# Gate and up products by one level of Strassen's scheme in an adaLN + convolution + GLU kernel

## Chip, cores and metric

The kernel runs on one core of one Trainium2 chip. The metric is the device time of one execution in microseconds (us); the median of three runs of the kernel before is 601.48 us (601.07 to 602.88). A core has five engines with a queue each, which run in program order and wait for one another by semaphores: TensorE (PE, matrix products into PSUM), VectorE (DVE), ScalarE (ACT), GpSimd (POOL, which has no access to PSUM here) and SyncE (SP), whose queue starts the DMA transfers.

## What is computed

One block of an adaptive-layernorm network on 2048 rows of 448 channels, all in fp32: a layernorm with a learned scale and shift, a gated long convolution, a second layernorm with scale and shift, and a gated linear unit (GLU) with 1792 inner columns.

```python
h = _layernorm(x) * (1 + ca) + sa
x = x + ga * conv_block(h, k, v, shift_k, ssm_k, ssm_D)
h = _layernorm(x) * (1 + cb) + sb
g = h @ w_gate            # 2048 x 448 times 448 x 1792
u = h @ w_up
x = x + gb * ((sigmoid(g) * u) @ w_down)     # 1792 x 448
```

The convolution is done by products with Fourier tables; it is the same in both kernels. The change concerns the last three lines.

## The kernel before

**Layout.** The GLU's rows come in four row blocks of 512 (`n` = 0 to 3), its inner columns in seven groups of 256 (`j`, NGRP = 7), each of two halves of 128 (`f`). The normalised rows are transposed on TensorE (`norm_turn`, L730), so that channels lie on partitions: 448 channels are three tiles of 128 and one of 64. A product is `weights (128 channels x 128 columns)` times `x (128 channels x 512 rows)` into a PSUM bank of 512 columns.

**Precision.** Every operand is split into two numbers of TensorE's fast fp32 format, hi and lo (hi = a rounded copy, made by ACT; lo = value - hi, made by DVE). A product is then hi*hi + lo*hi + hi*lo: three matmuls for a full tile. The tile of 64 channels holds its hi part in the lower and its lo part in the upper 64 partitions, beside weights that are there twice, and needs two. So a gate or an up block of 128 columns takes 3 x 3 + 2 = 11 matmuls.

**gate_up** (L755) does the 22 matmuls of gate and up for one (j, n, f) into a pair of banks (PSUM tag `t`, two pairs in turn), then ACT takes the sigmoid of gate out of PSUM (L768), DVE multiplies it by up out of PSUM (L769), and h is split (hi by ACT L772, lo by DVE L773). **down** (L776) does 12 matmuls per 256 rows of the product with w_down (tag `y`, one pair) and DVE adds them to the result `x1` (L790); on the last group the result is stored (L792).

**Order of work.** The program is written out by hand: within `manual_schedule` each engine gets its instructions in the order of the calls. At L862 the blocks (j, n) are listed; for each block the two halves of gate/up follow each other, and after each half comes one down call of the block before. `ends` (L845) names small jobs that follow a half: loads of the next weights (`load_w`), their splits (`split_hi` L489 on ACT, `split_lo` L497 on DVE), row statistics (`ln2_stats` L408), normalising of later row blocks (`norm_rows` L717). w_down is multiplied by the output scale gb on POOL (`gate_raw` L484). Just ahead of the GLU, the last output of the convolution is multiplied by the gate and added to x (`gate` L355: a product and a sum per quarter); of the second half's four quarters all are done by DVE, the last two between GLU blocks (L846, L847).

## Time and profile before

| | before |
|---|---|
| runs, median (lowest to highest) | 601.48 us (601.07 to 602.88) |
| profiled execution, span from first to last instruction | 602.7 us |
| TensorE clock granted, mean | 0.994 |
| instructions | 7614 |
| ACT busy | 41% |
| DMA | 51.87 MB, mean 86 GB/s |

The profiled execution has no time of its own beside its span; the span lies within the range of the three runs and 1.2 us above their median. The page of the profile lists busy time by engine, the chain of work that ended last and groups of instructions by source line; the timeline lists the instructions of an engine in order with start and duration. A group is named by what it writes and reads: gu is the PSUM tile of gate and up, d that of down, xt the transposed rows, wt the split weights, hh and hl the two parts of h, x the result. L numbers are lines of the kernel before.

### The profile page before, as it was taken

How to read it: one execution, taken by the hardware profiler on the slowest of the kernel's cores; microseconds unless marked ns; L12 is line 12 of the kernel's file. 1: busy time of each engine (PE TensorE's matmuls, PEld its weight loads, DVE VectorE, ACT ScalarE, POOL GpSimd, SP SyncE). 2: the span in 40 equal slices, each digit the busy share in tenths (PEclk: the TensorE clock that was granted, in tenths of full speed). 3: DMA queues.
4: the chain of work that ended last, by engine and by line, in shares of the span. 5: the costliest groups of instructions: out<-in, count | busy, mean ns of one | idle time of the engine just before them, and what ended most of it. 6: DMA issues, size and time to landing. Idle time of an engine off the chain costs nothing.

```text
span 602.7 us, 7614 instructions
## 1 busy us (share of the span) xinstructions
PE 572.8 (95%) x3100; PEld 437.2 (73%) x3100; DVE 319.1 (53%) x401; ACT 245.5 (41%) x429; POOL 80.0 (13%) x69
## 2 busy tenths in 40 slices
...
GB/s 284 264 298 306 241 210 301 181 226 189 165 21 48 18 1 1 0 1 0 67 35 32 35 36 1 30 36 35 2 30 37 34 5 27 2 1 30 61 62 91
DMA packets 36535, 51.87 MB, mean 86 GB/s; under 512 B 18451, under 2 KB 25365, under 8 KB 36373
## 3 DMA queue, kind: packets, MB, share of 16 engines
...
q14 instruction: 11, 0.08, 0.0%
...
## 4 chain that ended last, share of the span: by engine, by line
PE 75%; DVE 8%; ACT 7%; DMA 5%; issue 2%; SPq 2%; DVEq 0%; ACTq 0%
PE gu L764 44%; PE d L787 21%; DMA ak<-kdk 3%; PE sa L325 2%; DVE acc L238 2%; PE s2v L308 2%; SPq L187 1%; PE s2k L277 1%; PE s1k L198 1%; ACT ak L199 1%; DMA ssm<-in_ssm_dram 1%; ACT gbrow L433 1%; PE pt L736 1%; ACT ak L283 1%; ACT gbrow L432 1%
## 5 line engine op out<-in xcount | busy, mean ns | idle before, releaser
L764 PE MATMUL gu<-xt,wt 128*128 128x512 f32 x1232 | 290.3, 391 | 1.0 <-DVE xt L746 1.0
L764 PEld LDWEIGHTS gu<-xt,wt 128*128 128x128 f32 x1232 | 231.1, 188 | 47.0 <-DVE xt L746 1.2
L769 DVE TENSOR_TENSOR sg<-sg,gu 128x512 f32<-128x512 f32 x56 | 38.4, 685 | 185.0 <-ACT sg L768 184.9
L787 PE MATMUL d<-wt,hh 128*128 128x448 f32 x448 | 127.6, 366 | 2.7 <-DVE x L790 2.7
L768 ACT ACTIVATE sg<-gu 128x512 f32<-128x512 f32 x56 | 33.4, 597 | 236.6 <-PE gu L764 236.6
L787 PEld LDWEIGHTS d<-wt,hh 128*128 128x128 f32 x448 | 84.0, 188 | 12.5 <-issue 1.9
L787 PE MATMUL d<-wt,hl 128*128 128x448 f32 x224 | 81.9, 366 | 0.0
L790 DVE TENSOR_TENSOR x<-x,d 128x896 f32<-128x896 f32 (+1 forms) x57 | 60.5, 1063 | 5.7 <-PE d L787 5.7
L773 DVE TENSOR_TENSOR hl<-sg,hh 128x512 fp32r<-128x512 f32 x56 | 39.7, 709 | 39.1 <-ACT hh L772 39.1
L772 ACT ACTIVATE hh<-sg 128x512 fp32r<-128x512 f32 x56 | 35.4, 631 | 45.8 <-DVE sg L769 45.8
L486 POOL TENSOR_TENSOR r<-r,gbrow 128x448 f32<-128x448 f32 x10 | 11.5, 1153 | 313.1 <-DMA r<-in_wd_dram 306.8
L175 DVE STREAM_TRANSPOSE av<-av 128x896 f32<-128x896 f32 x24 | 44.5, 1881 | 4.9 <-ACT av L326 2.7
L787 PEld LDWEIGHTS d<-wt,hl 128*128 128x128 f32 x224 | 42.1, 188 | 3.3
L312 DVE TENSOR_TENSOR m<-s2v,ak 128x896 f32<-128x896 f32 x32 | 33.4, 1088 | 8.0 <-PE s2v L308 5.4
L308 PE MATMUL s2v<-av,w 64*64 64x448 f32 x256 | 33.2, 571 | 0.6 <-DVE av L175 0.5
L325 PE MATMUL sa<-m,wa 128*64 128x448 f32 x128 | 28.2, 562 | 2.6 <-ACT av L326 2.6
L325 PEld LDWEIGHTS sa<-m,wa 128*64 128x64 f32 x128 | 8.0, 140 | 22.1 <-issue 10.0
L308 PEld LDWEIGHTS s2v<-av,w 64*64 64x64 f32 x256 | 10.6, 138 | 17.5 <-issue 12.0
L277 PE MATMUL s2k<-ak,w 64*64 64x448 f32 x128 | 16.9, 578 | 3.7 <-DMA ak<-kdk 3.0
L326 ACT ACTIVATE av<-sa 128x896 f32<-128x896 f32 x16 | 14.5, 908 | 13.7 <-PE sa L325 13.7
L501 DVE TENSOR_TENSOR wt<-r,wt 128x512 fp32r<-128x512 f32 (+1 forms) x30 | 19.7, 662 | 0.0
L175 DVE STREAM_TRANSPOSE ak<-ak 128x896 f32<-128x896 f32 x8 | 14.0, 1867 | 10.0 <-ACT ak L199 10.0
...
## 6 DMA issues: line engine op xcount, KB each, us to landing
...
r<-in_wg_dram SPq DMA_DIRECT2D x10, 256.0 KB, 2.7
```

Source lines behind the costliest of these rows:

```text
L175: DVE.transpose(x, x)
L277: PE.matmul(pt[c:c + 64, b, :D], w2[r:r + 64, 0], x[r:r + 64, b], start=True, stop=True)
L308: PE.matmul(pts[b][c:c + 64, ex, :D], w2[r:r + 64, ex], x[r:r + 64, b], start=True, stop=True)
L312: DVE.tensor_mul(cols4(m[b], h, n), cols4(rows(pts[b]), h, n), k[:, b].unsqueeze(1).to_broadcast([P, 2, D // w, w]))
L325: PE.matmul(pt[r, b, :D], wa[:, b, r], m[b][:, ex], start=True, stop=True)
L764: PE.matmul(pgu[:, s], wts[j][s][k % 2][:, t, f * P:(f + 1) * P], x[:, xs], start=first, stop=not left)
L768: ACT.activation(sg, pgu[:, 0], AF.Sigmoid)
L769: DVE.tensor_mul(sg, sg, pgu[:, 1])
L772: ACT.activation(hh, sg, AF.Copy)
L773: DVE.tensor_sub(hl, sg, hh)
L787: PE.matmul(pt[:, i, :D], h[:, (2 * e + i) * P:(2 * e + i + 1) * P], w[:, f], start=m == 0, stop=m == len(ops) - 1)
L790: DVE.tensor_add(y, y, rows(pt)[:, a:b])
```

## The change

Gate and up are now done for a **pair** of row blocks at once. For the two halves of a column group, the two row blocks of a pair and two parts of the channels, a gate or up product is a 2 x 2 block product:

- A11, A12: weights of the first column half for channel part 1 (192 channels) and part 2 (256 channels); A21, A22: the same for the second half.
- B11, B21: the first row block's channels of part 1 and 2; B12, B22: the second row block's.

Strassen's scheme in Winograd's form takes seven products: A11B11, A12B21, S1T1, S2T2, S3T3, A22T4, S4B22, with S1 = A21 + A22, S2 = S1 - A11, S3 = A11 - A21, S4 = A12 - S2 and T1 = B12 - B11, T2 = B22 - T1, T3 = B22 - B12, T4 = B21 - T2. The parts are uneven; where one is narrower, the sums take its channels alone. Three products have part 1's 192 channels (one full tile and a packed 64: 3 + 2 = 5 matmuls), four have 256 (6 matmuls).

What goes with it:

- POOL forms the weight sums of each step (`w_sums`, five instructions) and, once per pair, the sums of x (`t_sum`). w_down is loaded and scaled whole (`gate_wd`).
- Each of the seven weight forms (128 x 512 numbers for both sides) is split into hi and lo in a ring of eight slots (`w_hi` on ACT, `w_lo` on DVE); the transposed rows exist in the forms B and T.
- The partial sums are put together out of PSUM by ACT (the copy `c1`) and DVE (`u2`, `u3`, `c1`), and gate and up are then multiplied from SBUF (`glu`); before, up came from PSUM.
- The first step (group 0 of the first pair) is done plainly (`plain_block`), while the sums for the next are made. There are 14 steps: 7 groups for each of 2 pairs.
- A fifth transposed tile per second row block of a pair gives channels in another position (`AT`, five columns in `cols`).
- The last three quarters of the convolution's gate go to POOL. The loads of the weights come from one array `wgu`; two small loads move from POOL's queue to ACT's; buffers are laid out anew.

The diff, cut to its core:

```diff
+    def gate_wd(j):
+        r = ring["wd", j]
+        POOL.tensor_mul(r, r, gbrow.unsqueeze(1).to_broadcast([P, 2, D]))
...
+    gate_wd(0)
...
+    def norm_rows(n, on_act=False, rows_=range(4)):
+        for i in rows_:
             g = slice(4 * n + i, 4 * n + i + 1)
-            if n == 0:
-                DVE.tensor_scalar(xn[:, i, :D], x1[:, i], rstd2[:, g], nmr2[:, g], op0=OP.mult, op1=OP.add)
-            else:
-                ACT.activation(xn[:, i, :D], x1[:, 4 * n + i], AF.Identity, bias=nmr2[:, g], scale=rstd2[:, g])
-        DVE.tensor_copy(xn[:, :, D:], xn[:, :, 384:D])
-        xns[n] = xn
-
-    xps = {}
-
-    def norm_turn(n, t0, tag="sa"):
-
-        xn = xns[n]
-        xps[n, t0] = pt = two(tag, f"pt{n}_{t0}")
-        for t in range(2):
+            parts = ((xn[:, i, 0:512].rearrange("p (h w) -> p h w", h=2)[:, :, 0:192], x1[:, 4 * n + i, 0:384].rearrange("p (h w) -> p h w", h=2)),
+                     (xn[:, i, 448:576], x1[:, 4 * n + i, 320:D]))
+            for o, x in parts:
+                if on_act:
+                    ACT.activation(o, x, AF.Identity, bias=nmr2[:, g], scale=rstd2[:, g])
+                else:
+                    DVE.tensor_scalar(o, x, rstd2[:, g], nmr2[:, g], op0=OP.mult, op1=OP.add)
+        if 3 in rows_:
+            DVE.tensor_copy(xn[:, :, 192:256], xn[:, :, 128:192])
...
+    def x_lo(name):
+        o, x = xf[name], x_src[name]
+        if o.shape[1] == 3:
+            DVE.tensor_sub(o[:, 2], x[:, 0], o[:, 0])
+            DVE.tensor_sub(o[64:128, 1], x[64:128, 1], o[64:128, 1])
+        else:
+            DVE.tensor_sub(o[:, 2:4], x, o[:, 0:2])
...
+    def t_sum(k):
+        if k == 1:
+            POOL.tensor_sub(full[:, 0:2], full[:, 4:6], full[:, 0:2])
+        if k == 3:
+            POOL.tensor_sub(full[:, 4], full[:, 6], full[:, 4])
+            POOL.tensor_sub(full[:, 5], full[:, 8], full[:, 5])
+        if k == 2:
+            POOL.tensor_sub(ts[:, 0, 0], full[:, 6], full[:, 0])
+            POOL.tensor_sub(ts[0:64, 0, 1], full[0:64, 7], full[0:64, 1])
+            POOL.tensor_copy(ts[64:128, 0, 1], full[64:128, 7])
+        if k == 4:
+            POOL.tensor_sub(ts[:, 1], full[:, 2:4], ts[:, 0])
+    F0, F1 = slice(0, P), slice(P, 2 * P)
+    def w_sums():
+        r = ring["raw"]
+        s1, s2, s3, s4 = sums
+        POOL.tensor_add(s1[:, 0:2], r[:, 2:5:2, :, F1], r[:, 0:2, :, F1])
+        POOL.tensor_add(s1[:, 2], r[:, 3, :, F1], r[:, 5, :, F1])
+        POOL.tensor_sub(s2, s1[:, 0:2], r[:, 2:5:2, :, F0])
+        POOL.tensor_sub(s3, r[:, 2:4, :, F0], r[:, 2:4, :, F1])
+        POOL.tensor_sub(s4, r[:, 0:2, :, F0], s2)
+    def w_src(name):
+        r = ring["raw"]
+        s1, s2, s3, s4 = sums
+        x = {"A11": r[:, 2:4, :, F0], "A12": r[:, 0:2, :, F0], "A22": r[:, 0:2, :, F1], "S1": s1[:, 0:3:2], "S2": s2, "S3": s3, "S4": s4}[name]
+        return x.rearrange("p t g f -> p g t f")
...
+    def w_hi(name, i):
+        forms[name, i] = slot(i).rearrange("p (s g t f) -> p s g t f", s=2, g=2, t=2)
+        ACT.activation(forms[name, i][:, 0], w_src(name), AF.Copy)
+    def w_lo(name, i):
+        x = forms[name, i]
+        DVE.tensor_sub(x[:, 1], w_src(name), x[:, 0])
...
+    def mms(pt, wh, x, start, stop):
+        if x.shape[1] == 3:
+            ops = [(0, 0, 0), (1, 0, 0), (0, 0, 2), (0, 1, 1), (1, 1, 1)]
+        else:
+            ops = [(0, 0, 0), (1, 0, 0), (0, 0, 2), (0, 1, 1), (1, 1, 1), (0, 1, 3)]
+        for m, (s, t, k) in enumerate(ops):
+            PE.matmul(pt, wh(s, t), x[:, k], start=start and m == 0, stop=stop and m == len(ops) - 1, skip_group_check=True)
+    def product(pt, name, i, xname, start, stop):
+        w = forms[name, i]
+        for g in range(2):
+            mms(pt[:, g], lambda s, t: w[:, s, g, t], xf[xname], start, stop)
+    def finish_h(k, h, fill=()):
+        hh, hl = [a1h[k][:, s] for s in range(2)]
+        ACT.activation(hh, h, AF.Copy)
+        for job in fill:
+            job()
+        DVE.tensor_sub(hl, h, hh)
+    def glu(y, fill=()):
+        ACT.activation(y[:, 0], y[:, 0], AF.Sigmoid)
+        for job in fill:
+            job()
+        DVE.tensor_mul(y[:, 0], y[:, 0], y[:, 1])
...
+    for i in range(1, 4):
+        gate(1, i, y_copy(1, i, y1[i]), POOL)
+    for dst in (slice(2, 4), slice(0, 2)):
+        load_gu(1, dst.start, dst.stop)
     norm_rows(0)
...
+    t_sum(1)
+    t_sum(2)
+    w_sums()
+    gate_wd(1)
...
+    plain_block("01", 0, ("B12", "B22"), st[0][:, 0])
+    down(0, 0, (hs["h11"], hs["h21"]), 0)
+    x_form("T2")
+    t_sum(3)
+    t_sum(4)
+    finish_h(hs["h12"], st[0][:, 0])
+    plain_block("01", 1, ("B12", "B22"), st[0][:, 1])
+    x_hi("T1")
+    w_hi("S1", 6)
+    x_lo("T1")
+    w_lo("S1", 6)
+    finish_h(hs["h22"], st[0][:, 1])
+    down(0, 0, (hs["h11"], hs["h21"]), 1)
+    w_form("S3", 0)
+    w_form("S4", 2)
...
+        if more:
+            w_sums()
+        if not first:
+            gate_wd(s)
+            pa = two("t", f"a{s}")
+            product(pa, "A11", at["A11"], "B11", True, True)
+            ACT.activation(c1, pa, AF.Copy)
+        hi("A11", 0)
+        do("a")
+        if not first:
+            dn(0, 0)
+        if not first:
+            lo("A11", 0)
+        do("b")
+        if more and not first and s + 2 < 2 * NGRP:
+            load_gu((s + 2) % NGRP, 2, 6)
+        hi("S2", 1)
+        pb_ = two("t", f"b{s}")
+        product(pb_, "S2", at["S2"], "T2", True, True)
+        DVE.tensor_add(u2, pb_, c1)
+        if not first:
+            lo("S2", 1)
+        do("c")
+        hi("S1", 2)
+        if not first:
+            dn(0, 1)
+        if not first:
+            lo("S1", 2)
+        do("d")
+        pc = two("sa", f"c{s}")
+        product(pc, "S1", at["S1"], "T1", True, True)
+        do("e")
+        hi("S3", 3)
+        if first:
+            dn(1, 0)
+        product(pb_, "S3", at["S3"], "T3", False, True)
+        DVE.tensor_add(u3, pb_, c1)
+        DVE.tensor_add(u3, u3, pc)
+        glu(u3, [lambda: lo("S3", 3), lambda: hi("A12", 4)])
+        dn(1, 1 if first else 0)
+        finish_h(new["h22"], u3[:, 0], [lambda: lo("A12", 4)])
+        do("f")
+        if not first:
+            product(pa, "A12", at["A12"], "B21", False, True)
+            h11 = u3[:, 0]
+            ACT.activation(h11, pa[:, 0], AF.Sigmoid)
+            DVE.tensor_mul(h11, h11, pa[:, 1])
+            finish_h(new["h11"], h11, [lambda: split_wd_hi(s)])
+        else:
+            split_wd_hi(s)
+            lo("A11", 0)
+        hi("A22", 5)
+        if not first:
+            dn(1, 1)
+        split_wd_lo(s)
+        if more:
+            load_wd(s + 1, wdraw)
+        do("g")
+        product(pb_, "A22", at["A22"], "T4", False, True)
+        DVE.tensor_add(c1, pb_, c1)
+        glu(c1, [lambda: lo("A22", 5), lambda: hi("S4", 6)])
+        if more and s + 2 < 2 * NGRP:
+            load_gu((s + 2) % NGRP, 0, 2)
+        finish_h(new["h21"], c1[:, 0], [lambda: lo("S4", 6)])
+        do("h")
+        if first:
+            lo("S2", 1)
+            load_gu(s + 2, 2, 6)
+        product(pc, "S4", at["S4"], "B22", False, True)
+        DVE.tensor_add(u2, u2, pc)
+        glu(u2)
+        finish_h(new["h12"], u2[:, 0])
+        do("i")
+        return new
...
+    jobs = {2: {"d": [do(ln2_stats, 8, 9)], "h": [do(ln2_stats, 10)]},
+            3: {"d": [do(ln2_stats, 11), do(stats_end, 2), do(ln2_stats, 12)], "f": [do(norm_rows, 2, True, (0, 1))], "g": [do(norm_rows, 2, True, (2, 3))], "h": [do(ln2_stats, 13)]},
+            4: {"b": [do(ln2_stats, 14)], "d": [do(ln2_stats, 15), do(stats_end, 3)], "e": [turn_of(2, (0, 1))], "h": [turn_of(2, (2, 3))]},
+            5: {"a": [do(norm_rows, 3, True, (0, 1))], "b": [do(norm_rows, 3, True, (2, 3))], "e": [turn_of(3, (0, 1))], "h": [turn_of(3, (2, 3))]},
+            1: {"i": [do(w_lo, "S1", 13)], "c": [do(x_form, "T3")], "d": [do(finish_h, hs["h21"], h11), do(x_form, "T4")]},
+            6: {"a": [do(x_hi, "B11")], "d": [do(x_lo, "B11")], "e": [turn_of(3, (4,)), do(t_sum, 1), do(t_sum, 2), do(t_sum, 3), do(t_sum, 4)],
+                "g": [do(x_hi, "T2")], "h": [do(x_lo, "T2"), do(x_hi, "T1")]},
+            7: {"a": [do(x_hi, "B21")], "b": [do(x_lo, "T1")], "c": [do(x_hi, "T3")], "d": [do(x_lo, "T3"), do(x_lo, "B21"), do(x_hi, "T4")], "e": [do(x_hi, "B22")], "f": [do(x_lo, "T4")], "g": [do(x_lo, "B22")]}}
+    for s in range(1, 2 * NGRP):
+        hs = step(s, hs, jobs.get(s, {}))
+    for n, ks in ((0, ("h11", "h21")), (1, ("h12", "h22"))):
+        for e in range(2):
+            down(2 * NGRP - 1, 2 + n, [hs[k] for k in ks], e, True, n == e == 1, ("y", "t", "t", "sa")[2 * n + e])
```

Here `hi` and `lo` are `w_hi` and `w_lo` for the next step's forms, `dn` is one down call of the step before, `st` holds the partial sums, `slot` and `form` places of the ring, and `do("a")` and so on run the jobs listed for a step.

398 lines of the change are left out of this document (211 added, 187 removed).

## The prediction

> **What bounds the kernel now.** The first view is the head of the profile's page. The span is 602.7 us, and TensorE (PE) is busy for 95% of it, VectorE (DVE) for 53%, GpSimd (POOL) for 13%.
>
> ```profile
> span 602.7 us, 7614 instructions
> PE 572.8 (95%) x3100; PEld 437.2 (73%) x3100; DVE 319.1 (53%) x401; ACT 245.5 (41%) x429; POOL 80.0 (13%) x69
> ```
> An average over unlike stages decides nothing, so the second view cuts the span into windows of 15 us. From about 210 us to the end every window reads like this one: PE 15.00 of 15.00 us at granted clock 1.00, DVE 6.09, ScalarE (ACT) 3.64, POOL nothing.
>
> ```profile
> core 0: us, PE busy (x) PEld busy (x) DVE busy (x) ACT busy (x) POOL busy (x), PEclk, DMA share, GB/s
> 330.00:345.00 15.00, 15.00 (x70) 12.90 (x70) 6.09 (x9) 3.64 (x7) 0.00 (x0) 1.00 0.13 35
> ```
> The third view is the chain of work that ended last. From 172.29 us on it is almost only gate/up matmuls (gu, L764) and down matmuls (d, L787).
>
> ```profile
> 172.29 15.27 PE gu L764 x66
> ...
> 322.76 5.00 PE gu L764 x22
> 327.76 2.43 PE d L787 x12
> ...
> 590.73 1.01 DVE x L790
> ...
> 594.62 1.10 DVE x L790
> 595.77 2.72 PE d L787 x12
> ```
> 22 gu matmuls take 5.00 us, so one is worth 0.2273 us; 12 down matmuls take 2.43 us, 0.2025 each. (The means of the grouped lines, 391 and 366 ns, overlap; the pitch is what counts.) Counts come from the lines grouped by form: 1232 gu and 448 + 224 = 672 down.
>
> ```profile
> L764 PE MATMUL gu<-xt,wt 128*128 128x512 f32 x1232 | 290.3, 391 | 1.0 <-DVE xt L746 1.0
> L787 PE MATMUL d<-wt,hh 128*128 128x448 f32 x448 | 127.6, 366 | 2.7 <-DVE x L790 2.7
> L787 PE MATMUL d<-wt,hl 128*128 128x448 f32 x224 | 81.9, 366 | 0.0
> ```
> Three more rows give the transposes and the end: 16 transposes in 1.97 us (0.123 each); the last matmul ends at 598.11 + 0.37 = 598.5, and 4.2 us of adding and storing follow.
>
> ```profile
> 169.32 1.97 PE L736 MATMUL pt<-ident,xn 128*128 128x128 f32 x16
> ...
> 598.11 0.37 PE L787 MATMUL d<-wt,hl 128*128 128x448 f32 x1
> 598.51 1.15 DVE L790 TENSOR_TENSOR x<-x,d 128x448 f32<-128x448 f32 x2 [2.80 <-PE d L787]
> ```
> The stage lasts 598.5 - 172.3 = 426.2 us. Its work is 1232 x 0.2273 = 280.0, 672 x 0.2025 = 136.1 and 48 transposes (16 of 64 lie ahead of it) = 5.9: 422.0. So PE idles for only 4.2 us here: **TensorE's work is the time**, and only fewer matmuls or new idling can move it.
>
> **What is removed.** A channel block costs 3 matmuls per 128 full channels and 2 for a packed 64. Before, one output is 3 x 3 + 2 = 11; a pair of row blocks with two column halves and two sides (gate, up) makes 88. After, a product over the 192-channel part costs 5, over the 256-channel part 6. Three of the first kind (A11B11, S1T1, S3T3) and four of the second (A12B21, S2T2, A22T4, S4B22) make 39, times two sides 78. There are 14 pair-groups; the first stays plain. 88 + 13 x 78 = 1102, which is 130 fewer, **-29.5 us**. Down stays at 672. Two more transposed tiles of four blocks cost 8 x 0.123 = +1.0. New PE work: 250.5 + 136.1 + 6.9 = 393.5. If PE never waited, the last matmul would end at 172.3 + 393.5 = 565.8 and the span at 570.0, 32.7 us less. So the change has **32.7 us of waiting to spend**.
>
> **What is added, per step** (one group of 256 columns, one pair). Prices:
>
> ```profile
> L790 DVE TENSOR_TENSOR x<-x,d 128x896 f32<-128x896 f32 x55 | 59.4, 1079 | 2.9 <-PE d L787 2.9
> L773 DVE TENSOR_TENSOR hl<-sg,hh 128x512 fp32r<-128x512 f32 x56 | 39.7, 709 | 39.1 <-ACT hh L772 39.1
> L772 ACT ACTIVATE hh<-sg 128x512 fp32r<-128x512 f32 x56 | 35.4, 631 | 45.8 <-DVE sg L769 45.8
> L768 ACT ACTIVATE sg<-gu 128x512 f32<-128x512 f32 x56 | 33.4, 597 | 236.6 <-PE gu L764 236.6
> L352 ACT ACTIVATE tmp<-y 128x896 f32<-128x896 f32 x7 | 6.3, 919 | 3.9 <-PE y L346 3.9
> L501 DVE TENSOR_TENSOR wt<-r,wt 128x448 fp32r<-128x448 f32 x10 | 6.2, 618 | 0.0
> L456 POOL TENSOR_TENSOR G<-G,arow 128x896 f32<-128x896 f32 x8 | 16.9, 2106 | 0.4
> L486 POOL TENSOR_TENSOR r<-r,gbrow 128x448 f32<-128x448 f32 x10 | 11.5, 1153 | 313.1 <-DMA r<-in_wd_dram 306.8 <-issue 6.3
> ```
> DVE with two inputs: 617 ns for 448 elements (L501) and 1079 for 896, so 1.03 ns per element; 512 take 0.69, 1024 about 1.22, in a sequence 0.08 less (the next starts before the last one's end). Per step it does five 1024-wide sums out of PSUM (5.7 us), four down adds (4.0), seven low halves of the weight forms, four of h, four gating products (15 x 0.61 = 9.2) and one low half of w_down (1.0): 19.9 us. ACT: seven high halves, four sigmoids, four of h, a 1024 copy (from 919 at 896: about 1.02) and w_down's: 10.0. POOL: 1153 ns for 448 and 2106 for 896, 2.13 ns per element; `w_sums` is four of 512 (1.29 each) and one of 256 (0.75), `gate_wd` 2.1: 8.0. PE needs 78 x 0.2273 + 48 x 0.2025 = 27.5. So in a plain step every engine has room, DVE 7.6 us. All this added work is priced at nothing there, hidden under PE's 27.5; if an engine needs more, PE waits. Loads: 1.5 MB of gate/up and 0.46 MB of w_down per step on SP; the nearest row lands 256 KB in 2.7 us. Everything is asked for a step ahead, so I take nothing; were it bound, the bound is one load of 1 MB, some 6 to 10 us, once.
>
> ```profile
> r<-in_wg_dram SPq DMA_DIRECT2D x10, 256.0 KB, 2.7
> ```
> **Where it does not hide: DVE and POOL exclude each other.** The timelines of both engines show it.
>
> ```profile
> 96.28 2.08 POOL L457 TENSOR_TENSOR G<-G,brow 128x896 f32<-128x896 f32 x1
> 97.15 1.23 DVE L441 TENSOR_TENSOR nmr<-nmr,rstd 128x4 f32<-128x4 f32 x1
> L441 DVE TENSOR_TENSOR nmr<-nmr,rstd x4: 161/164/1232, 91.5 to 125.1; 128x4 f32<-128x4 f32 x4
> ...
> 181.30 1.16 POOL L486 TENSOR_TENSOR tmp<-tmp,gbrow 128x448 f32<-128x448 f32 x1 [14.17 <-DMA tmp<-in_wd_dram]
> 181.40 1.61 DVE L773 TENSOR_TENSOR hl<-sg,hh 128x512 fp32r<-128x512 f32 x1 [0.70 <-ACT hh L772]
> ...
> 162.22 3.09 POOL L486 TENSOR_TENSOR tmp<-tmp,gbrow 128x448 f32<-128x448 f32 x2 [2.51 <-ACT gbrow L398]
> 163.10 1.21 DVE L360 TENSOR_TENSOR x<-x,G 128x896 f32<-128x896 f32 x1
> ```
> L441 multiplies four numbers and takes 0.16 us, but the one at 97.15 took 1.23: it ended at 98.38, with POOL's instruction (96.28 + 2.08 = 98.36). L773 takes 0.69, but 1.61 under POOL's at 181.30. At 163.10 DVE waits about 0.1 for the first of two POOL products, and then the second waits for DVE: 3.09 us for two that take 1.15 each. Each has two SBUF inputs. A DVE instruction fed from PSUM shows none of this. Of the new DVE work the low halves and gating products (15 per step, w_down's included) have two SBUF inputs, and the kernel before had nearly no POOL work in this stage.
>
> I walked the five queues instruction by instruction in program order: one starts when its engine is free, its inputs are done (0.03 us after ACT or DVE, 0.2 after PE, 0.1 to PE) and, for these two kinds, the other engine's instruction is over. Idle PE time, in us, by step (step 0 is the plain group):
>
> | | start | 0 | 1 | 2-6 | 7 | 8-12 | 13 and end | sum |
> |---|---|---|---|---|---|---|---|---|
> | no exclusion | -0.3 | 0.5 | 0.0 | 5.2 | 4.8 | 0.2 | 1.6 | 12.0 |
> | DVE goes first | 0.7 | 3.1 | 7.9 | 12.8 | 9.7 | 0.2 | 1.6 | 36.0 |
> | turns | 0.7 | 7.6 | 5.2 | 12.3 | 10.9 | 0.2 | 1.6 | 38.5 |
>
> How the entries arise. **Start:** `gate_wd(0)` is one POOL product of 2.1 us from 162.2, so DVE's x += G waits until 164.2 instead of 163.2; +1.0, less 0.3. **Steps 0 and 1:** POOL has 12.6 us of gates (six of 2.1, on DVE before), then T1, T2, the weight sums, w_down, T3, T4 (18.2 us without a pause), then step 1's sums. DVE's splits of B12, B22, T2, T1 come between, each waiting for a POOL instruction; T3, needed by S3T3, is some 4 to 7 us late. PE waits for it, behind it stands the rest of step 1. **Steps 2 to 6:** layernorm statistics, and DVE behind by 1 to 2 us, so PE waits for the `y` bank that a down add holds (dn(0,1), dn(1,1)). **Step 7:** the second pair's forms (T1, T3, B21, T4, B22) make DVE 25.8 us of a 27.5 us step; it already starts late because step 6's T sums, 10.7 us on POOL, collided with it; PE waits for T1, T3 and B22. **Steps 8 to 12:** DVE's waits fall into its slack. **End:** 1.6 before the last h21; the old 1.4 us waits for `y` are gone (its four groups have banks of their own).
>
> What stays uncertain is how much of the exclusion lands on PE: below, 12 us of idling (none lands), above, 38.5 and more. I take the mean of the two lower rows, 37, being nearest to the rows above, which show full exclusion: 570.0 + 37 = **607**, against 602.7. The runs' median 601.48 lies 1.2 below that span, so **606** in device time.
>
> Which DVE instructions are excluded is the next question. L722 scales 448 elements with one input, four in 1.78 us, 0.45 each, against 605 ns for one-input L417:
>
> ```profile
> 167.66 1.78 DVE L722 TENSOR_SCALAR xn<-x,rstd,nmr 128x448 f32<-128x448 f32 x4 [0.21 <-DVE nmr L426]
> L417 DVE BATCH_NORM_STATS2 st<-x 128x6 f32<-128x448 f32 x12 | 7.3, 605 | 0.1
> ```
> No row shows such a fast copy or scaling beside POOL; I let them run free. By the Trainium skill, page "SBUF — State Buffer", section "Who interferes with whom", copies, casts and tensor_scalar in their two-port mode also contend with GpSimd, and the loser blocks for a whole instruction. No run here shows that; by it, the sum would be that of the third rival.
>
> **The rivals.**
> *The waits land in slack* (faster). DVE's waits cost PE only where DVE has no lead; if it enters each stage a few us ahead of my walk, none shows: 570.0 + 12 = 582, device time 581. For it: steps 8 to 12 carry the same collisions free. Against: steps 0, 1 and 7 have no slack to land in. It decides once PE idles under 31 us.
> *Half land*: idling 24, 594 span, 593. For: every wait I counted is a few us late at most, and a different turn order removes it.
> *Scalings and casts wait too* (slower). At the start DVE's row normalisations and the B11 casts stand between POOL's six gates of 2.1 us: first gu at 173.5 (DVE first) to 179.1 (turns) instead of 172.3; walking on, idling is 40 to 44: span 610 to 614, 611 in device time. Against: the wait is unseen here.
> *It does not cut what it says*: if gu stayed near 1232, the same waits would give 636. The counting leaves no room; it sits in the rest.
>
> **How the numbers follow.** My forecast, 606 (own range 600 to 609), has chance 0.38; slack 0.22; half 0.20; scalings 0.15; the rest (a late load, more waits) 0.05. A measurement tells about 0.3%, 1.8 us, from no change: 0.07 of the forecast's chance lies inside that. Faster 0.22 + 0.20 = 0.42; same 0.07; slower 0.31 + 0.15 + 0.05 = 0.51. The range is 583 to 614: about 0.1 of the slack case lies below, and the rest with a little more above.
>
> **What would show it.** In the changed profile: 1102 gate/up matmuls at 0.227 us pitch; windows of steps 8 to 12 with PE full and DVE near 11 of 15; POOL near 4.4 of 15. DVE two-input instructions stretched beside POOL's show the exclusion; PE waits on DVE for T3 and T1 in steps 1 and 7 show its price. First gu at 173 rather than 179 says that scalings run free. It is wrong if PE idles under 31 us in all, or if steps 8 to 12 are not PE-bound, which I hold for sure.

## The result and the profile after

| | before | after |
|---|---|---|
| runs on one chip, median (lowest to highest) | 601.28 us (600.48 to 602.88) | 621.12 us (618.79 to 623.67) |
| profiled span | 602.7 us | 621.9 us |
| ratio to before | | 1.0326, 95% interval 1.0291 to 1.0361 |

The changed kernel is slower by 3.3%, some 20 us. The forecast of 606 us had the direction right and the size wrong; 621 lies outside its range. L numbers from here on are lines of the changed kernel, and of a variant where its rows are shown. In the new rows, a, b and c are PSUM tiles of the seven products, ring holds the split weights, sum POOL's weight sums, st the partial sums, full the transposed rows before their split, and inb first the gated outputs, later the raw weights. The head of the page after:

```profile
span 621.9 us, 7744 instructions
PE 563.4 (91%) x2986; PEld 419.5 (67%) x2986; DVE 497.2 (80%) x553; ACT 303.4 (49%) x505; POOL 226.3 (36%) x152
```

PE has 114 instructions fewer and is busy for 91% instead of 95%; the trace counts 1102 gate and up matmuls instead of 1232, as forecast. DVE went from 53% to 80%, POOL from 13% to 36%. The windows of the first gate/up products show where a part of the time went; the third column from the end is the granted clock:

```profile
core 0: us, PE busy (x) PEld busy (x) DVE busy (x) ACT busy (x) POOL busy (x), PEclk, DMA share, GB/s
165.00:180.00 15.00, 9.19 (x81) 5.50 (x77) 14.25 (x18) 5.37 (x12) 9.19 (x5) 0.85 0.22 72
180.00:195.00 15.00, 11.73 (x46) 9.75 (x47) 11.63 (x22) 7.15 (x14) 5.56 (x3) 0.70 0.00 0
195.00:210.00 15.00, 12.56 (x62) 9.38 (x60) 14.62 (x17) 9.21 (x14) 9.15 (x6) 0.98 0.45 171
```

Before, these windows had PE at a clock of 1.00. Here PE is partly idle and its clock falls to 0.70. The timelines of DVE, POOL and PE say what stands there:

```profile
166.25 2.19 DVE L368 TENSOR_TENSOR x<-x,inb 128x896 f32<-128x896 f32 x1
171.69 11.79 DVE L745 TENSOR_SCALAR xn<-x,rstd,nmr 128x384 f32<-128x384 f32 x8
```

```profile
165.40 2.09 POOL L488 TENSOR_TENSOR tmp<-tmp,gbrow 128x896 f32<-128x896 f32 x1 [2.54 <-ACT gbrow L406]
172.74 2.08 POOL L367 TENSOR_TENSOR inb<-inb,tmp 128x896 f32<-128x896 f32 x1 [5.25 <-ACT tmp L360]
174.89 2.08 POOL L368 TENSOR_TENSOR x<-x,inb 128x896 f32<-128x896 f32 x1
176.93 2.19 POOL L367 TENSOR_TENSOR inb<-inb,tmp 128x896 f32<-128x896 f32 x1
179.19 2.07 POOL L368 TENSOR_TENSOR x<-x,inb 128x896 f32<-128x896 f32 x1
181.22 2.18 POOL L367 TENSOR_TENSOR inb<-inb,tmp 128x896 f32<-128x896 f32 x1
183.48 2.16 POOL L368 TENSOR_TENSOR x<-x,inb 128x896 f32<-128x896 f32 x1
```

```profile
177.25 0.33 PE L757 MATMUL pt<-ident,xn 128*128 128x128 f32 x1 [1.60 <-DVE xn L745]
181.53 0.47 PE L757 MATMUL pt<-ident,xn 128*128 128x128 f32 x1 [3.96 <-DVE xn L745]
183.75 2.82 PE L757 MATMUL pt<-ident,xn 128*128 128x128 f32 x12 [1.74 <-DVE xn L747]
186.24 4.07 PE L860 MATMUL gu<-x,ring 128*128 128x512 f32 x11
```

The eight scalings that normalise the first rows (L745) take 11.79 us, while POOL runs its six gate operations of 2.1 us one behind the other. A scaling gets in only between two of POOL's operations: the last five end at 174.90, 177.19, 179.20, 181.48 and 183.49, each 0.1 to 0.2 us behind the end of one of POOL's (174.82, 176.97, 179.12, 181.26, 183.40); the first three, begun before POOL's, take 0.34 to 0.48 each. PE waits 1.60, 3.96 and 1.74 us for them, and the first gu matmul starts at 186.24 instead of 172.29. At 166.25 the sum x += G takes 2.19 instead of 1.21 us, because it waits for the gating of w_down.

In the steps, the group of down matmuls carries the largest wait of PE, 12.9 us for the down add (L882):

```profile
L879 PE MATMUL d<-wd,h 128*128 128x448 f32 x672 | 150.0, 373 | 13.1 <-DVE x L882 12.9
L846 DVE TENSOR_TENSOR h<-st,h 128x512 fp32r<-128x512 f32 x56 | 50.0, 892 | 19.5 <-ACT h L843 18.2
```

One instance, at the head of step 3, in the timelines of POOL, DVE and PE:

```profile
282.20 1.29 POOL L801 TENSOR_TENSOR sum<-inb 128x512 f32<-128x512 f32 x1 [16.59 <-DMA inb<-in_wgu_dram]
283.45 1.20 POOL L802 TENSOR_TENSOR sum<-inb 128x256 f32<-128x256 f32 x1
284.60 1.29 POOL L803 TENSOR_TENSOR sum<-sum,inb 128x512 f32<-128x512 f32 x1
```

```profile
282.34 1.70 DVE L852 TENSOR_TENSOR st<-st 128x512 f32<-128x512 f32 x1 [0.70 <-ACT st L849]
284.74 1.69 DVE L846 TENSOR_TENSOR h<-st,h 128x512 fp32r<-128x512 f32 x1 [0.70 <-ACT h L843]
286.35 1.07 DVE L882 TENSOR_TENSOR x<-x,d 128x896 f32<-128x896 f32 x1
```

```profile
287.48 4.26 PE L879 MATMUL d<-wd,h 128*128 128x448 f32 x12 [1.98 <-DVE x L882]
```

POOL's weight sums start at 282.20, when their weights have landed. DVE's GLU product (L852) and low half (L846) take 1.70 and 1.69 us, against 0.69 alone: 2.0 us lost. The down add behind them is 2 us late, and the next down product, which needs the add's PSUM banks, waits 1.98 us. Its 12 matmuls then take 4.26 us where the timeline mostly shows 2.6 to 2.7; the granted clock from 287.5 to 291.7 is 0.59.

**The account.** Four stretches of PE's timeline, cut at the start of the modulation's last matmuls (mod, L391, products that make the scales and shifts from the condition; at 160.07 in this profile), the first gu matmul, the first A11 product of step 2, that of step 8 and the end of the last matmul. All profiles of this study are cut the same way, so that a late attention part does not count. "Thin" means one column wide. The medians come from several chips; the ratio to the kernel before on the same chip stands with each experiment. A profile is of one execution and not of the median one (e3's took 615.1 us, e12's 605.59). e16 differs from the changed kernel ahead of the GLU alone, so the distance of its row from that of after, up to 1.5 us in a stretch, tells how far one profile can be trusted.

| profile (us) | to first gu | steps 0, 1 | steps 2-7 | steps 8-end | runs' median |
|---|---|---|---|---|---|
| before | 15.4 | 426.2 to the end | | | 601.28 |
| after | 26.2 | 61.2 | 191.8 | 178.1 | 621.12 |
| e16 tables on POOL | 26.2 | 60.1 | 191.4 | 176.6 | 619.93 |
| e1 gates on DVE | 17.1 | 67.4 | 193.9 | 176.7 | 621.03 |
| e2 scalings on ACT | 23.5 | 61.4 | 191.2 | 176.9 | 620.47 |
| e3 sums thin | 26.1 | 58.2 | 185.0 | 182.3 | 612.49 |
| e5 all sums on DVE | 21.5 | 60.4 | 210.4 | 196.7 | 652.93 |
| e6 POOL later | 26.2 | 61.0 | 194.3 | 175.8 | 622.86 |
| e7 = e1 + e6 | 17.3 | 67.8 | 195.5 | 175.8 | 620.67 |
| e9 PE kept busy | 27.4 | 60.6 | 194.0 | 176.8 | 621.89 |
| e10 POOL thin from step 1 | 26.2 | 57.0 | 177.3 | 175.7 | 601.23 |
| e11 DVE's low halves thin | 26.1 | 59.8 | 172.5 | 175.6 | 599.87 |
| e8 = e10 + e11 | 26.2 | 58.2 | 169.2 | 175.6 | 592.63 |
| e13 gates thin | 17.5 | 60.1 | 190.6 | 180.0 | 612.14 |
| e14 first sums thin | 26.2 | 50.7 | 191.4 | 178.4 | 613.03 |
| e12 = e13 + e14 | 17.4 | 50.5 | 194.7 | 176.9 | 601.73 |
| e15 = e8 + e12 | 16.5 | 50.4 | 169.3 | 175.5 | 576.57 |

### The profile page after: what moved, and what is told of

Same layout as the page of the kernel before. It is cut to its first block, busy times and chain, and to the rows that moved or that the text cites. A ratio compares the mean times of both kernels' runs of the same rounds, so it can differ in the third digit from the quotient of the medians.

```text
span 621.9 us, 7744 instructions
## 1 busy us (share of the span) xinstructions
PE 563.4 (91%) x2986; PEld 419.5 (67%) x2986; DVE 497.2 (80%) x553; ACT 303.4 (49%) x505; POOL 226.3 (36%) x152
## 4 chain that ended last, share of the span: by engine, by line
PE 45%; DVE 27%; ACT 14%; DMA 5%; issue 5%; SPq 2%; POOL 1%; DVEq 0%; ACTq 0%; POOLq 0%
PE d L879 12%; PE b L834 9%; PE c L834 6%; PE a L834 4%; DVE x L882 4%; DMA ak<-kdk 3%; DVE ring L821 2%; DVE st L852 2%; DVE h L846 2%; PE sa L333 2%; ACT h L843 2%; DVE xn L745 2%; ACT st L849 2%; PE gu L834 2%; PE s2v L316 2%
## 5 line engine op out<-in xcount | busy, mean ns | idle before, releaser
L879 PE MATMUL d<-wd,h 128*128 128x448 f32 x672 | 150.0, 373 | 13.1 <-DVE x L882 12.9
L879 PEld LDWEIGHTS d<-wd,h 128*128 128x128 f32 x672 | 126.2, 191 | 32.1 <-DVE x L882 19.3
L834 PE MATMUL b<-xt,ring 128*128 128x512 f32 x442 | 108.5, 392 | 3.0 <-DVE xt L774 2.4
L834 PEld LDWEIGHTS b<-xt,ring 128*128 128x128 f32 x442 | 82.5, 188 | 20.8 <-DVE xt L774 3.3
L801 POOL TENSOR_TENSOR sum<-inb 128x512 f32<-128x512 f32 x12 | 16.7, 1390 | 213.0 <-DMA inb<-in_wgu_dram 186.3
L834 PE MATMUL a<-x,ring 128*128 128x512 f32 x286 | 69.4, 390 | 0.0
L882 DVE TENSOR_TENSOR x<-x,d 128x896 f32<-128x896 f32 (+1 forms) x57 | 60.4, 1063 | 7.4 <-PE d L879 7.4
L846 DVE TENSOR_TENSOR h<-st,h 128x512 fp32r<-128x512 f32 x56 | 50.0, 892 | 19.5 <-ACT h L843 18.2
L834 PEld LDWEIGHTS a<-x,ring 128*128 128x128 f32 x286 | 53.5, 188 | 10.7
L843 ACT ACTIVATE h<-st 128x512 fp32r<-128x512 f32 x56 | 35.4, 632 | 32.8 <-DVE st L852 21.7
L821 DVE TENSOR_TENSOR ring<-sum,ring 128x512 fp32r<-128x512 f32 x52 | 42.5, 818 | 1.6 <-ACT ring L817 1.4
L852 DVE TENSOR_TENSOR st<-st 128x512 f32<-128x512 f32 x39 | 31.3, 803 | 12.8 <-ACT st L849 10.6
L834 PE MATMUL c<-x,ring 128*128 128x512 f32 x156 | 38.0, 391 | 1.6 <-DVE x L777 1.6
L1033 DVE TENSOR_TENSOR st<-b,st 128x1024 f32<-128x1024 f32 x13 | 15.9, 1221 | 23.4 <-PE b L834 23.4
```

The source lines that it names most:

```text
L821: DVE.tensor_sub(x[:, 1], w_src(name), x[:, 0])
L834: PE.matmul(pt, wh(s, t), x[:, k], start=start and m == 0, stop=stop and m == len(ops) - 1, skip_group_check=True)
L843: ACT.activation(hh, h, AF.Copy)
L846: DVE.tensor_sub(hl, h, hh)
L852: DVE.tensor_mul(y[:, 0], y[:, 0], y[:, 1])
L879: PE.matmul(pt[:, i, :D], h[:, (2 * e + i) * P:(2 * e + i + 1) * P], x, start=m == 0, stop=m == len(ops) - 1)
```

## The experiments

Two theories stand against each other. (The expectations add rivals for single runs: Q, that the start is late because of the convolution's end and the transfers; G and S, that what goes from the start with the gates is gained, or is lost again in steps 0 and 1.) **P**: DVE and POOL take turns at operations that both read from SBUF, and PE pays for the turns. **R**: DVE's own work and the order of its queue are the limit, and POOL's part in it is small. A third, **C**, says that PE's lower clock behind each wait costs on its own.

**e1: the gates back on DVE.**

```diff
-    for i in range(1, 4):
-        gate(1, i, y_copy(1, i, y1[i]), POOL)
+    yc = [y_copy(1, i, y1[i]) for i in range(1, 4)]
...
+    gate(1, 1, yc[0], DVE)
...
+    gate(1, 2, yc[1], DVE)
...
+    gate(1, 3, yc[2], DVE)
```

> The changed kernel with the last three quarters of the convolution's gate back on VectorE, between its other work. Theory P (GpSimd and VectorE exclude each other by turns, scalings and casts included): the eight row scalings of the first row block fall from 11.8 us to about 2.5, the first gate/up matmul comes 8 to 10 us earlier, some 2 us of slow TensorE clock go too: 609 to 612 us. Rival Q (the start is late because of the convolution's end and the transfers): the first matmul moves by under 2 us, 619 to 622 us.

Measured: 621.03 us, ratio 1.0317 (1.0278 to 1.0355), no gain; the time is Q's, but the first gu matmul does come 9.1 us earlier, 17.1 behind the modulation instead of 26.2, where Q allowed 2. But steps 0 and 1 take 67.4 instead of 61.2 us, and steps 2 to 7 2.1 more. The two late gates now meet POOL's T sums, as the timelines of DVE, POOL and PE and a window show:

```profile
188.88 3.14 DVE L368 TENSOR_TENSOR x<-x,inb 128x896 f32<-128x896 f32 x1
193.62 2.17 DVE L367 TENSOR_TENSOR inb<-inb,tmp 128x896 f32<-128x896 f32 x1
```

```profile
188.62 2.45 POOL L785 TENSOR_TENSOR full<-full 128x1024 f32<-128x1024 f32 x1 [21.28 <-PE a L834]
193.11 1.72 POOL L791 TENSOR_TENSOR xn<-full 64x512 f32<-64x512 f32 x1
```

```profile
193.75 4.38 PE L834 MATMUL a<-x,ring 128*128 128x512 f32 x11 [3.47 <-DVE ring L821]
```

```profile
195.00:210.00 15.00, 11.13 (x26) 7.07 (x25) 14.84 (x11) 1.74 (x3) 14.92 (x9) 0.61 0.28 105
```

The gate's sum takes 3.14 us where 1.1 is its own time, the split of A12 comes late, PE waits 3.47 us for it, and the next window runs at a clock of 0.61. The gates went to another engine, and the turns came back elsewhere.

**e2: the first scalings on ACT.**

```diff
-    norm_rows(0)
+    norm_rows(0, True)
```

> The changed kernel with the eight row scalings of the first row block on ScalarE, which takes 0.5 to 0.7 us for each; the gates stay on GpSimd. P: scalings take some 4.5 us and wait for nobody, but the one copy, the two casts and the subtractions still meet GpSimd: first matmul 4 to 7 us earlier, 614 to 617 us. Rival Q, or a rival in which GpSimd is not the reason and VectorE's scalings are slow by themselves with their split rows: the second would give the same gain or more, since nothing waits, and then the copy and the casts would show no stretch.

Measured: 620.47 us, ratio 1.0302 (1.0263 to 1.034). The start is 2.7 us shorter, where 4 to 7 and 614 to 617 us were expected. ACT does the eight scalings in 4.03 us, but then two casts on DVE stand beside POOL's last two gate operations (183.40 to 187.71):

```profile
183.51 4.48 DVE L767 CAST x<-full 128x512 fp32r<-128x512 f32 x2 [2.08 <-ACT full L762]
```

The same two take 0.43 us each in e12, where POOL is free. So casts from SBUF to SBUF wait for POOL as the scalings do. The copy ahead of them (L747) takes 0.93 us here, and 0.28 in the changed kernel, where it begins 0.07 us ahead of POOL's next operation.

**e3: the sums thin.** It leaves out most of the weight sums after the first set and of the second pair's T sums.

```diff
+        if len(calls) > 1:
+            r, s1, s2, s3, s4 = [x[..., 0:129:128] if x is r else x[..., 0:1] for x in (r, s1, s2, s3, s4)]
...
+        if len(tcalls) > 4:
+            w = slice(0, 1)
```

> The changed kernel with GpSimd's sums of weights (after the first call) and of rows (second pair) one column wide instead of 128 or 512; the sums beyond that column are stale, so part of the computation is left out. GpSimd's time per step falls from 8 to about 3 us (the scaling of w_down stays). P: TensorE's idle time after the first matmul falls from 23 to 11 to 14 us, the slow clock behind the long gaps mostly with it: 606 to 612 us; VectorE's subtractions fall back to 0.69 us. Rival R (VectorE has simply too much to do, GpSimd is beside the point): under 3 us gained.

Measured: 612.49 us, ratio 1.0158 (1.0102 to 1.0214). It gains 9 us, half a microsecond less than P's range asked for, and yet PE still waits 1.1 to 2.5 us at the head of most steps. POOL's next operation, the gating of w_down, has moved up to where the sums were:

```profile
277.68 2.12 POOL L488 TENSOR_TENSOR wdraw<-wdraw,gbrow 128x896 f32<-128x896 f32 x1
```

```profile
277.74 2.61 DVE L871 TENSOR_TENSOR h<-st,h 128x512 fp32r<-128x512 f32 x1 [0.70 <-ACT h L868]
```

The low half of 0.69 us takes 2.61. In this profile the stretch from step 8 on, nearly free of waits before, even became slower (182.3 instead of 178.1); two of the four runs were 5 us shorter than the profiled one, so this may not hold for them.

**e5: no POOL in the GLU.** The gates as in e1, and all sums and the gating of w_down on DVE.

```diff
-        POOL.tensor_add(s1[:, 0:2], r[:, 2:5:2, :, F1], r[:, 0:2, :, F1])
+        DVE.tensor_add(s1[:, 0:2], r[:, 2:5:2, :, F1], r[:, 0:2, :, F1])
...
```

> As the first of these, and all of GpSimd's sums and scalings in this stage on VectorE, which needs about half of GpSimd's time for each and gets 3.7 us more per step: about 23.6 of 27.5. P: nobody waits for the port, steps 8 to 12 stay bound by TensorE, waits remain in steps 2 to 7: 592 to 602 us. Rival R (VectorE's queue is the bound): 610 us or more, as its load goes up.

Measured: 652.93 us, ratio 1.085 (1.0818 to 1.0882). P alone, which expected a gain, failed here. No turns are left, and PE waits more, at the same place as before, up to 5.6 us at a time:

```profile
254.89 4.85 PE L879 MATMUL d<-wd,h 128*128 128x448 f32 x12 [5.59 <-DVE x L882]
```

The sums stand at the head of the step in DVE's queue, ahead of the down add that PE needs next. So P is not the whole: what counts is how late DVE is at the adds, for whatever reason.

**e6 and e7: POOL's work of a step later.** From step 2 on a copy of one column lets POOL begin only behind the first down add; e7 has e1's gates as well.

```diff
             dn(0, 0)
+            POOL.tensor_copy(mark, x1[:, 4 * pn0, 0:1])
+            if more:
+                w_sums()
+            gate_wd(s)
```

> From step 2 on, POOL's six operations at a step's head (the five weight sums and the gating of W_down, together some 9.8 us) are let go only when DVE has done the step's first down add; a copy of one column on POOL reads what that add wrote. No work of DVE, ACT or PE changes. Theory P (a POOL operation with two inputs and a DVE operation with two inputs take turns, and it costs where it meets the tail of a step: GLU product, low half, down add, with 0.69 us ones stretched to 1.7): the second down product's waits of 1.6 to 2.7 us in steps 2 to 7 go, about 8 us, and with them the matmuls at half speed right behind them, some 3 us: 608 to 614 us. Theory R (DVE has too much work in steps 0 to 7, wherever POOL's work lies): DVE does the same, so 619 to 623 us.

> The gates of the second half are back on DVE (as in e1) and POOL's work of each step from 2 on waits for the first down add (as in e6). P: if what e1 gained at the start was only given back to the same waits in the steps, both gains add: 598 to 606 us. If the first step itself gives it back (its waits and its half clock at 195 to 210), the start is worth nothing and this is like the other: 608 to 614 us. R: 618 to 623 us.

Measured: 622.86 us (1.0331, 1.0307 to 1.0355) and 620.67 us (1.0305, 1.0288 to 1.0323). Neither gained. In e6 PE's waits are only in other places:

```profile
318.46 1.16 ACT L817 ACTIVATE ring<-sum 128x512 fp32r<-128x512 f32 x2 [4.17 <-POOL sum L803]
```

```profile
319.12 1.11 DVE L821 TENSOR_TENSOR ring<-sum,ring 128x512 fp32r<-128x512 f32 x1 [2.08 <-ACT ring L817]
```

```profile
321.38 1.06 PE L757 MATMUL pt<-ident,xn 128*128 128x128 f32 x8 [1.61 <-POOL sum L805]
```

```profile
419.61 4.07 PE L834 MATMUL b<-xt,ring 128*128 128x512 f32 x8 [3.62 <-DVE xt L774]
```

The third row names POOL's sum, which no transpose reads; what PE needs there is the bank that DVE's down add, over at 321.23, holds. That add stands in DVE's queue behind a low half, whose high half on ACT waited 4.17 us for POOL's late sum. In steps 2 to 7 DVE's idle time ahead of the low halves of the weights is 9.5 us in e6 and 1.4 in the changed kernel. So e6 moves the turns away from the head of a step and adds waits for late data, and it does not tell the two apart: P's narrower form, that the turns cost because they meet the tail of a step before, got no support, and is not refuted.

**e8, e10, e11: a square of four.** Leaving out POOL's work from step 1 on (e10), DVE's low halves of weights, h and w_down from about step 2 on (e11), or both (e8). The cut-down operations are one column wide. P alone asked for 601 to 605 in e10 and 604 to 610 in e11, R for 609 to 613 and 592 to 598.

```diff
+        if len(los) > 9:
+            DVE.tensor_sub(x[:, 1, :, :, 0:1], w_src(name)[..., 0:1], x[:, 0, :, :, 0:1])
...
+        if j > 1:
+            POOL.tensor_mul(r[:, 0, 0:1], r[:, 0, 0:1], gbrow[:, 0:1])
+            return
```

> Leaves out part of the computation: from about step 2 on DVE's low halves of the weights, of h and of W_down, and POOL's weight sums and gating of W_down, are done one column wide, and the second pair's T sums too. PE's matmuls are all there. DVE is left with adds, GLU products and x splits, well under half its time. If the scheme cuts PE's work as it says (393.5 us of matmuls from the first gu), the stage from the first gu of 186 then ends near 186 + 393.5 + 8 for the waits and the slow clock of the first steps that stay = 588 to 594, with 3 behind it: 591 to 600 us. If the products themselves take longer than counted (a rival: the matmuls do not run at 0.227 us in this order), 608 us or more. The difference to the whole kernel is what DVE and POOL cost in steps 2 to 12.

> Leaves out part of the computation: from step 1 on POOL's weight sums and its gating of W_down, and the second pair's T sums, are one column wide, so POOL has next to nothing to do after 225 us. DVE's, ACT's and PE's work is whole. With the run that thinned DVE's low halves too (592.6 us) and the whole changed kernel (621.1) this makes a square of four. P (each of DVE's losses in steps 2 to 7 is a turn taken by POOL): steps 2 to 6 take 27.5 to 28.5 us instead of 29.9 to 32.2, step 7 about 31 instead of 36.7, in all 16 to 20 us less: 601 to 605 us. R (DVE's own work and the order of its queue): as in e3, where the gating alone was left on POOL, or a little less: 609 to 613 us.

> The other corner of the square; leaves out part of the computation: from about step 2 on DVE's low halves of the weights, of h and of W_down are one column wide, POOL's work is whole. P alone: POOL's 10 us bursts still meet DVE's adds and GLU products, so half of the waits stay: 604 to 610 us. R: DVE has 4 to 6 us in each step to spare and the turns cost nothing: 592 to 598 us. If the two are one thing (the turns matter only because DVE has no slack, and the slack is small only because of the turns), both corners lie near the run with both thinned.

Measured: e8 592.63 us (0.9837, 0.9818 to 0.9855), e10 601.23 (1.0005, 0.9992 to 1.0018), e11 599.87 (0.9981, 0.9965 to 0.9997). One window of the whole kernel and of the three, with the busy times of PE, PE's weight loads, DVE, ACT and POOL:

```profile
300.00:360.00 60.00, 56.01 (x266) 47.25 (x265) 47.07 (x58) 34.44 (x57) 17.99 (x12) 1.00 0.21 68
```

```profile
300.00:360.00 60.00, 59.24 (x286) 50.44 (x285) 45.49 (x62) 33.41 (x55) 1.93 (x12) 1.00 0.24 74
```

```profile
300.00:360.00 60.00, 59.13 (x286) 50.27 (x285) 36.83 (x63) 33.67 (x55) 16.55 (x12) 1.00 0.24 74
```

```profile
300.00:360.00 60.00, 60.00 (x292) 51.70 (x291) 33.05 (x62) 34.40 (x56) 3.83 (x18) 1.00 0.23 74
```

In these 60 us PE issues 266 instructions in the whole kernel and 286, 286 and 292 in the three others. In steps 2 to 7 taking POOL away saves 14.5 us, taking DVE's low halves away 19.3, both 22.6: the two gains overlap. With POOL's work gone, 8.1 of the 22.6 us stay (177.3 - 169.2), and these are DVE's own work; with the low halves gone, 3.3 stay (172.5 - 169.2). So e10 comes out as P says, e11 between the two, and neither theory holds alone: the turns cost PE time where DVE has little slack left, and DVE has little partly because of the turns.

**e9: PE kept busy at the start.** 94 transposes of the identity, of no use, fill PE's waits for the scalings.

```diff
+            PE.transpose(idle[:, 0, 0:P], ident, ident)
```

> Adds 94 transposes of the identity (no use is made of them) on PE between the last projection of the attention part and the transposes of the first normalised rows, where PE waits for the stretched scalings at 175 to 184 us; everything else as in the changed kernel. Theory C (idle PE gets a lower clock for the next stretch, granted 0.70 at 180 to 195 and 0.79 at 210 to 225, and the first plain block runs slower for it): the first plain blocks end 2 to 4 us earlier and the time is 617 to 619 us. If the clock costs nothing because the first step waits for DVE anyway: 620 to 622 us.

Measured: 621.89 us, ratio 1.0311 (1.0289 to 1.0332). The clock stays up:

```profile
165.00:180.00 15.00, 13.65 (x139) 11.32 (x136) 13.43 (x17) 5.08 (x12) 11.52 (x6) 1.00 0.11 38
180.00:195.00 15.00, 14.29 (x86) 12.16 (x85) 10.81 (x24) 8.00 (x15) 3.78 (x2) 1.00 0.00 1
```

It is 1.00 in both windows instead of 0.85 and 0.70, and step 2 begins no earlier (88.0 us behind the modulation against 87.4). At the start the slow clock is hidden behind DVE. C falls for this stretch; in steps 2 to 7 it was not tested.

**e12, e13, e14: POOL's work of the start.** One column wide are the gates (e13), the first four T sums, two sets of weight sums and one gating of w_down (e14), or all of it (e12). In e12, e14 and e15 four extra loads fill the buffers that the sums would have written.

```diff
+        if h == 1 and i > 0:
+            eng.tensor_mul(pairs(gg)[:, :, 0:1], pairs(gg)[:, :, 0:1], y[:, :, 0:1])
...
+        if len(calls) <= 2:
...
+        if len(tcalls) <= 4:
```

> Leaves out part of the computation: POOL's work between 170 and 235 us (three gates of the second half, the first four T sums, the first two sets of weight sums, the gating of W_down for group 1) is one column wide; afterwards all is whole. Theory P at the start: the eight scalings take 2.7 us instead of 11.8, the first gu matmul comes 15 us behind the modulation's matmuls instead of 26, and step 2 begins 68 to 74 us behind them instead of 87: 602 to 609 us. Theory R at the start (the stretch from the modulation to step 2 is held by DVE's own chain of normalising, splitting and adding, and POOL's turns fall into its slack): step 2 begins 82 to 86 us behind: 615 to 620 us.

> Leaves out part of the computation: the six gate operations of POOL at 172 to 186 us are one column wide; everything else is whole. With e12, which thinned all of POOL's work of that stretch and gained 19.4 us, this splits the stretch in two. G (the gates against the scalings alone, 9 to 11 us at the first gu matmul): step 2 begins 76 to 78 us behind the modulation's matmuls instead of 87: 609 to 612 us. S (what is gained at the first gu is lost again in steps 0 and 1 to the T sums and weight sums, as when the gates went to DVE): 84 us behind and 617 to 620 us.

> The other half; leaves out part of the computation: the first four T sums, the first two sets of weight sums and the gating of W_down for group 1 are one column wide; POOL's gates are whole. If the two halves add: the first gu matmul stays 26 us behind the modulation's, the stretch from it to step 2 falls from 61.3 to 52 to 54 us, and the time is 611 to 614 us. If the halves stand in for each other (S): about 618 us, and only taking both away brings the 19.4 us.

Measured: e12 601.73 us (1.0028, 0.9998 to 1.0059), e13 612.14 (1.0184, 1.013 to 1.0238), e14 613.03 (1.0168, 1.0133 to 1.0203). The same eight scalings in e12:

```profile
171.79 2.68 DVE L754 TENSOR_SCALAR xn<-x,rstd,nmr 128x384 f32<-128x384 f32 x8
```

2.68 us instead of 11.79. The gates cost 8.7 us before the first gu matmul, the sums 10.5 us in steps 0 and 1; they add, 1.4 and 1.6% of before's time on the same chip beside 3.0% for both. e1 gained nothing because it put the gates on DVE among the T sums; with the gates' work gone, the first gain stays.

**e15: everything thin.** e8 and e12 together.

> e8 and e12 together; leaves out part of the computation: POOL's work from 170 us on, and DVE's low halves from about step 2 on, are one column wide. All of PE's matmuls are there. If the two gains add (28.5 us of waits in the steps, 19.4 at the start): 572 to 576 us, beside 570 that the matmuls alone were counted at. If something else of the changed kernel holds PE: 580 us or more.

Measured: 576.57 us, ratio 0.9571 (0.9551 to 0.9592), half a microsecond above the 572 to 576 expected. From the first gu matmul, at 175.97, to the end of the last one at 571.11:

```profile
175.97 1.20 PE L909 MATMUL gu<-x,ring 128*128 128x512 f32 x4 [0.51 <-DVE x L779]
```

```profile
569.73 1.38 PE L928 MATMUL d<-wd,h 128*128 128x448 f32 x6
```

395.1 us, where the matmuls were counted at 393.5. The scheme cuts what it says, and what the whole kernel loses against it is 45.7 us in the account above (457.3 against 411.6).

**e4: POOL work in the kernel before.** Three idle products in each half block from group 2 on.

```diff
+        if j > 1:
+            for _ in range(3):
+                POOL.tensor_mul(dummy, dummy, gbrow)
```

> The kernel before with three idle POOL products of 128x448 added in each half block from group 2 on (nothing uses them), some 6 us of POOL in each 14. Of the kernel before DVE is busy 38% of the steps and PE never waits for it, so theory P's turns fall into slack: 601 to 604 us, with DVE's operations stretched on the page. If two-input POOL work slows PE or DVE in another way as well: 606 us or more. Its attention part is that of the kernel before, so its modulation matmuls (156.9 us in the one profile of before) show whether that time moves from run to run by itself (up to 2 us either way) or whether the change's 157.1 to 162.3 us is later than before's.

Measured: 605.22 us, ratio 1.0083 (1.0053 to 1.0113), 1.2 us above what was expected at most. On its page the low halves take longer than the 709 ns of before:

```profile
L779 DVE TENSOR_TENSOR hl<-sg,hh 128x512 fp32r<-128x512 f32 x56 | 50.5, 902 | 39.2 <-ACT hh L778 39.2
```

PE hardly waits for them: its stage lasts 427.3 us, 1.1 more than before's 426.2, which e17 and e18 repeat. DVE is busy for 109 of the 260 us from 300 on, POOL for 153. So POOL work beside a DVE that is busy for under half the time is nearly free, as the square said. Another 2.0 us come ahead of the first gu matmul, where the clearing of the idle products' tile delays a gating of w_down into the scalings:

```profile
166.17 2.97 DVE L722 TENSOR_SCALAR xn<-x,rstd,nmr 128x448 f32<-128x448 f32 x4 [1.11 <-PE mod L405]
```

They take 2.97 us here and 1.78 before, 1.2 of the 2.0: the scalings wait for POOL in this kernel too. The medians on this chip differ by 4.5 us (605.22 against 600.72); what the profile does not show of that stays open.

**e16, e17, e18: ahead of the GLU.** After's modulation starts 3.2 us later than before's, at a wait for the convolution's transfers. e16 undoes the change's one edit there that moves instructions to another queue, e17 makes it in the kernel before, e18 is the kernel before again.

```diff
-    ACT.dma_start(sk, shift)
-    ACT.dma_start(cv, cvec)
+    POOL.dma_start(sk, shift)
+    POOL.dma_start(cv, cvec)
```

> The changed kernel with one of the change's edits ahead of the GLU undone: the two small loads at the very beginning are issued from POOL's queue again instead of ACT's. In every run of the changed kernel and its variants so far the modulation's last matmuls start at 157.1 to 162.3 us (15 profiles, mean 159.0), in the kernel before at 156.9 and in its variant e4 at 154.6. If the edit delays the attention part: 154 to 157 us here, and 618 to 620 us in all. If not: 157 to 161 and 620 to 622.

> The kernel before with only that edit: the two small loads are issued from ACT's queue. If the edit costs what the two kernels differ by ahead of the GLU: the modulation's last matmuls at 157 to 160 us and 603 to 605 us in all. If not: 154 to 157 and 601 to 602.

> The kernel before, unchanged, for a second profile of it. If its modulation's last matmuls start at 156 to 157 us again, the changed kernel is later by 2 to 3 us ahead of the GLU for a reason of its own; if that time moves by itself over several us, as it does between profiles of the changed kernel, the 3.2 us between the two first profiles are partly chance.

Measured: e16 619.93 us (1.0288, 1.0245 to 1.0331), e17 602.81 (1.001, 0.999 to 1.003), e18 603.18 in its one run. The wait, in the timelines of PE of before, after, e16 and e17:

```profile
96.00 1.02 PE L277 MATMUL s2k<-ak,w 64*64 64x448 f32 x3 [3.05 <-DMA ak<-kdk]
```

```profile
100.15 1.02 PE L285 MATMUL s2k<-ak,w 64*64 64x448 f32 x3 [7.48 <-DMA ak<-kdk]
```

```profile
98.35 1.01 PE L285 MATMUL s2k<-ak,w 64*64 64x448 f32 x3 [4.98 <-DMA ak<-kdk]
```

```profile
95.03 1.02 PE L277 MATMUL s2k<-ak,w 64*64 64x448 f32 x3 [2.16 <-DMA ak<-kdk]
```

The edit is not the cause: e16 still has a long wait, 4.98 us, and e17 a short one, 2.16. The modulation's start is 154.6 to 156.9 us in four profiles of the kernel before and its variants (mean 155.5), and 157.1 to 162.3 in sixteen of the changed kernel and its variants (mean 159.0). So the change costs some 3.6 us there by itself, and single profiles scatter by 2 to 3 either way. What in it does so, the new places of the buffers or another thing, stays open.

## Why the prediction was wrong

**Right: the cut in PE's work.** Counted at 393.5 us, measured as 395.1 in e15.

**Right: that DVE and POOL exclude each other. The size in the steps came out partly by luck.** Against e15, steps 0 and 1 lose 10.8 us (61.2 - 50.4), predicted 11.0 to 12.8; steps 2 to 7 lose 22.5 (191.8 - 169.3), predicted 22.5 to 23.2; steps 8 to the end 2.6, predicted 1.8. The sum is 35.9, and the prediction's two lower rows without their start give 35.3 and 37.8. But these rows are idle time of PE, and of that the trace records only 5.0, 15.9 and 2.0 us in the three stretches, 22.9 in all. Most of the rest is the clock, which the prediction did not price: some 5 us in steps 0 and 1 (granted 0.66 from 186.3 to 190.3 and 0.79 from 210 to 225) and 3.6 in steps 2 to 7 (0.94 in two windows of 30 us), both estimates from those windows; some 4 are short losses that no row names. So the sum came out with waits that were too long and a clock that was missing. With the 10.8 us by which the first gu matmul is late, PE's waiting is 33.7, above the 31 that the prediction gave as its limit. Steps 8 to 12 are bound by PE as forecast: from 450 to 560 us it is busy for 108.9 of 110, DVE for 11.8 of every 15 (forecast 11), POOL for 5.2 (4.4). The waits for T3 in steps 1 and 7 and for B22 are there, and none for T1 shows:

```profile
235.85 0.49 PE L834 MATMUL b<-xt,ring 128*128 128x512 f32 x1 [0.70 <-DVE xt L774]
421.90 0.50 PE L834 MATMUL b<-xt,ring 128*128 128x512 f32 x1 [1.72 <-DVE xt L774]
436.91 2.57 PE L834 MATMUL c<-x,ring 128*128 128x512 f32 x10 [1.59 <-DVE x L777]
```

They are 0.70, 1.72 and 1.59 us, where the walk had T3 of step 1 late by 4 to 7; most of the rest is the down adds' 12.9.

**Wrong: "No row shows such a fast copy or scaling beside POOL; I let them run free."** This is the step that failed. The start was given 0.7 us; measured are 26.2 - 15.4 = 10.8. Of these 8.7 go with POOL's gates (17.5 are left in e13), where the scalings take 11.79 us, and 2.67 without them; of the other 2.1, the sum x += G waiting for the gating of w_down is 1.0, as predicted, and about 0.9 is that the change's eight smaller scalings take 2.67 us even alone, where four took 1.78. By the Trainium skill, page "SBUF — State Buffer", section "Who interferes with whom", tensor_scalar, casts and copies in their two-port mode can contend with GpSimd, and the loser blocks for a whole instruction; the trace agrees, 11.79 against 2.67 us, and 4.48 against 0.86 for the two casts of e2. The prediction had this rule as a rival, with chance 0.15. "First gu at 173 rather than 179 says that scalings run free" was the right test: it came at 186.24, or 183.1 without the 3.2 us of the attention part.

**Wrong also: the size in that rival.** It had the mechanism but put the first gu matmul at 179.1 at most and the span at 610 to 614. Taking turns with POOL's operations of 2.1 us, one scaling to each, cost 4.0 us more than its walk (183.1 against 179.1).

**Not priced: the attention part.** It starts the modulation 3.2 us later in this profile, 3.6 in the mean; the cause stays open.

The sum by the prediction's own terms: 570.0, + 1.6 for PE's work, + 3.2 + 10.8 ahead of the first gu matmul, + 35.9 of losses in the stage is 621.5, beside the span of 621.9. With 10.8 instead of 0.7 us for the start alone, its 606 would have been 616.

The other rivals: the waits did not land in slack, nor half of them. "It does not cut what it says" is refuted by e15.
